# Delta-rule attention and feed-forward on one core: one join product per block, half as many fill transfers, and the Gram steps at a block's first slot

## The chip, the cores and the metric

The kernel runs on one core of a Trainium2 chip. The metric is the device time of one execution in microseconds, as the median of three runs. Five engines work side by side: TensorE (PE in the profile; its weight loads are PEld), VectorE (DVE), ScalarE (ACT), GpSimd (POOL) and SyncE (SP), which here only issues transfers.

## The reference

Four sequences of 768 steps with eight heads of size 48 go through a delta rule; its output, 3072 rows of 384, goes through a feed-forward of width 2048.

```python
for t in range(S):
    kt, vt, bt = (k_n[:, :, t], v[:, :, t], beta[:, :, t, None])
    y[:, :, t] = np.einsum('bhd,bhde->bhe', q[:, :, t], state)
    v_old = np.einsum('bhde,bhd->bhe', state, kt)
    state = state + bt[:, :, :, None] * np.einsum('bhd,bhe->bhde', kt, vt - v_old)
...
h = x @ w_in
g = np.maximum(0.01 * h, h)
return (g @ w_out).astype(np.float32)
```

## The kernel before

The 768 steps are cut into 12 blocks of 64 steps (`C`); a block holds 32 problems (8 heads x 4 sequences), handled as two groups `g` of 16. For block n the kernel does, in this order:

- `gram(n)`: products of the keys with the keys and queries (`pg`, L282) for each g. ScalarE copies the key part to `gs` (L286), from where eight transfers write it to `gd` in DRAM (L290) and two read it back as `L` (L306), problems on partitions. VectorE masks the query part into `rq` (L297) and copies the quadrant that joins the two halves of a problem into `gm` (L303).
- `inv(n)`: VectorE takes the norms from `L` (L323 to L332) and eliminates (L347, L352: some 122 small instructions) to the inverses of the two 32-step halves, tile `T`. ScalarE makes a second layout (L401, "the T copy"); transfers write both layouts to DRAM (`td` L408, `tt` L409).
- `solve(n)`: `merge_z` reads the inverses back: four transfers into `rt` (L461), and 16 fills of 16 KB that place 32x32 pieces on the diagonals of `sa` (L465) and `sb` (L468), two tiles for each g. The join product is `pz` (L436, from `gm` and `sa`), scaled to `zs` (L471), then in `merge_u` `pu` (L436, from `sb` and `zs`), copied into `rt` (L490). Then `pk` (L553), `pw` (L569), `pc` (L579, carries the state on) and `py` (L589), whose result `ys` (L591) is the block's output.
- `columns(n)`: TensorE transposes `ys` to `px` (L619); ScalarE and VectorE split it into `xh` and `xl` (L120, L121).
- `ffn(n)`: 16 slots f, each nine matmuls `ph` (L648), `gh` on ScalarE (L653), a second activation in place (L654), `gl` on VectorE (L656), and later six matmuls `po` (L638). At the block's end `po` is copied to `ob` (L668, in the same three buffers as `ys`) and stored (L671).

While the feed-forward of block n runs, `weave` traces the steps of later blocks between its slots: solve(n+1), inv(n+2) and gram. A tuple (stream, steps, a, b) spreads the steps from slot a to slot b. A scheduler then sets the final order of each engine's queue, with `behind(...)` as constraints; so the order on the engines is not the order of the source. All transfers that matter here stand in one queue, SP's, in order: one that waits holds all behind it.

Blocks 0 and 1 share one inverse and go another way. Tiles `cg` hold converted weights in block 0 and later `sa` and `sb`. `ps_a` gives four PSUM banks to all small products.

A "block" below is the stretch between two `pn` matmuls (L509), the first instruction of each solve from block 2 on; they stand at 142.06, 197.08, 245.39, ... 540.77 and 586.83 us.

Of the kernel before, what the change touches and what calls it, by code (L numbers as in the profile page):

```python
# [39 lines left out]
KQ_BUFS = 2  # L40
KT_BUFS, Q_BUFS = 2, 4
GM_BUFS = 4
YT_BUFS = 2
R0 = 64


# [1 line left out]
def delta_moe_kernel(ctx: ExitStack, tc, kq0, kqT, kv, qT, beta, cst, w_all, out, nblk):  # L48
# [86 lines left out]
    def weights():  # L135

        for f in range(NFC):
            words = raws.pop(f).bitcast(U32).rearrange("p (n two) -> p two n", two=2)  # L140
            lo, hi = words[:, 0], words[:, 1]
            g = sb.tile([P, 2 * DO], F32, tag="cg", name=f"cg{f}", bufs=CB)
            gi = g.bitcast(U32)
            with behind("S" if f < KA else "xh"):
                nc.scalar.activation(g, hi.bitcast(F32), AF.Abs)
            with behind("mask" if f < KA else f"gl{f - AG}" if f"gl{f - AG}" in mark else "x"):
                i = nc.vector.tensor_scalar(g, g, HI_MIN, HI_MAX, ALU.max, ALU.min)
            mark["work"] = i.ins
            if f + WAHEAD >= WEARLY:
                load_w(f + WAHEAD, "work")  # L150
            nc.vector.tensor_scalar(gi, gi, 3, 0x3FFFFFF8, ALU.logical_shift_left, ALU.bitwise_and)
            nc.vector.scalar_tensor_tensor(gi, hi, 0xC0000000, gi, ALU.bitwise_and, ALU.bitwise_or)
# [106 lines left out]
    def gram(n):  # L259
        need(sv, solve, n - Q_BUFS // NGR)  # L260
        kqs = []
        for g in range(NGR):
            t = sb.tile([P, GS, NPAIR, 2, C], F32, tag="kq", name=f"kq{n}_{g}", bufs=KQ_BUFS)
            kqs.append(t)
            with behind("kq"):
                for b in range(2):
                    nc.sync.dma_start(t[b * R0:b * R0 + D].rearrange("p s u x t -> p (s u x t)"), kqT[n, g, b])
        b0 = where[n][0]
        Lh[b0] = sb.tile([P, HC, HC], F32, tag="L", name=f"L{b0}", bufs=2)
        gd = dr.tile([64, HC, HC], F32, tag="gd", name=f"gd{n}")  # L270
        for g in range(NGR):
            kq = kqs[g]
            gs = sb.tile([P, 2, NPAIR, C], F32, tag="gs", name=f"gs{n}_{g}", bufs=2)
            gm[n, g] = m = sb.tile([P, NPAIR, HC], F32, tag="gm", name=f"gm{n}_{g}", bufs=GM_BUFS)

            ps = [ps_a.tile([P, 512], F32, tag="a", name=f"pg{n}_{g}_{b}") for b in range(2)]
            pv = [x.rearrange("p (u x t) -> p x u t", u=NPAIR, x=2) for x in ps]
            for p in range(NPAIR):
                for c in range(2):
                    for b in range(2):  # L280
                        r = slice(b * R0, b * R0 + D)
                        nc.tensor.matmul(ps[b][c * 64:(c + 1) * 64, p * 128:(p + 1) * 128],  # L282
                                         kq[r, c ^ b, p, 0], kq[r, c ^ b, p].rearrange("p x t -> p (x t)"),
                                         start=True, stop=True)
            for b in range(2):
                nc.scalar.copy(gs[:, b], pv[b][:, 0])  # L286
            for c in range(2):
                for e in range(2):
                    a = e * HS + g * GH + c * GU
                    nc.sync.dma_start(  # L290
                        gd[a:a + GU].rearrange("l j i -> j l i"),
                        gs[c * 64 + e * HC:c * 64 + (e + 1) * HC].rearrange("p b u t -> p (b u) t")[:, :, e * HC:(e + 1) * HC])
            qa = of("q", n, g)
            for b in range(2):
                for c in range(2):
                    r = slice(c * 64, (c + 1) * 64)
# [127 lines left out]
    def square(x, g):

        if (x, g) not in squares:
            squares[x, g] = t = sb.tile([P, NPAIR, P], F32, tag="cg", name=f"{x}{g}", bufs=CB)
            nc.vector.memset(t, 0.0)
        return squares[x, g]

    def product(n, g, name, lhs, rhs):

        ps = ps_a.tile([P, 512], F32, tag="a", name=f"{name}{n}_{g}")
        with behind("po"):
            for i in range(NPAIR):
                nc.tensor.matmul(ps[i * HC:(i + 1) * HC, 0:P], lhs[:, i], rhs[:, i], start=True, stop=True)  # L436
        return ps[:, 0:P]

    def merge_z(n, g, t):

        T, Tt = Tts[n]
        if n < 2:
            if n:
                for e in (1, 0):
                    place(n, g, e)
            gt = gm[n, g].rearrange("p c u i -> p (c u) i")
            pz = ps_a.tile([P, 512], F32, tag="a", name=f"pz{n}_{g}")
            zv = pz[:, 0:GU * HC].rearrange("p (u t) -> p u t", u=GU)
            lo = slice(R0 + HC, P)
            with behind("po"):  # L450
                for u in range(GU):
                    for h in range(2):
                        nc.tensor.matmul(zv[h * 64:h * 64 + HC, u], gt[lo, u // NPAIR * GU + h * NPAIR + u % NPAIR],
                                         t[lo, h, u // NPAIR, u % NPAIR, HC:], start=True, stop=True)
            zs[n, g] = z = sb.tile([P, 2, GU, HC], F32, tag="yt", name=f"zs{n}_{g}", bufs=YT_BUFS)
            for h in range(2):
                nc.scalar.copy(z[n * 64:n * 64 + HC, h], zv[h * 64:h * 64 + HC])
            return
        gl = slice(g * GH, (g + 1) * GH)
        for e in (1, 0):  # L460
            nc.sync.dma_start(half_of(n, g, e).rearrange("p h u i -> p (h u) i"), T[e, :, gl])  # L461
        A, B = square("sa", g), square("sb", g)
        for k in range(NPAIR):
            r = slice(k * HC, (k + 1) * HC)
            nc.sync.dma_start(A[r, :, r], Tt[gl].rearrange("(k v) i m -> k i v m", k=NPAIR)[k])  # L465
        for v in range(NPAIR):
            r = slice(v * HC, (v + 1) * HC)
            nc.sync.dma_start(B[r, :, r], T[1, :, gl].rearrange("m (k v) i -> v m k i", k=NPAIR)[v])  # L468
        pz = product(n, g, "pz", gm.pop((n, g)), A)
        zs[n, g] = z = sb.tile([P, NPAIR, HC], F32, tag="yt", name=f"zs{n}_{g}", bufs=YT_BUFS)  # L470
        nc.scalar.mul(z.rearrange("p k (m e) -> p k e m", e=2), pz.rearrange("p (k e m) -> p k e m", k=NPAIR, e=2), -1.0)  # L471
# [321 lines left out]
```

## Time and profile before

| what | value |
|---|---|
| median of 3 runs | 665.0 us (664.61 to 666.47) |
| the profiled execution | 666.35 us, of it span 664.6 us |
| busy share of the span | PE 92%, PEld 85%, DVE 68%, ACT 51%, POOL 2% |
| TensorE's granted clock, mean | 0.986 |
| largest shares of the chain that ended last | `ph` 31%, `po` 29% |
| seven blocks from 197.08 to 540.77 us | 343.69 us, PE busy in 336.47 |

The busy time is a sum over stages with different limits, so single stretches of the timeline are what counts. Successive matmuls overlap: a row's second number is a duration, and what one costs is the distance to the next one's start. A matmul in full float32 shows as two records.

### The profile page before, as it was taken

The numbers are of one execution on the slowest core, as the hardware profiler recorded it, in microseconds if no ns is written. First come the engines' busy times: TensorE is split into PE (matmuls) and PEld (weight loads), VectorE is DVE, ScalarE is ACT, GpSimd is POOL, SyncE is SP. The second block draws the span as 40 slices with busy tenths as digits, with TensorE's granted clock in tenths as the row PEclk, the third lists the DMA queues.
The fourth block names the chain that finished last, engine by engine and source line by source line (L and its number), as shares of the span: only waits on it lengthen the run. The fifth ranks groups of instructions, "written<-read, shape, count | busy, mean of one in ns | idle before, by whom it ended". The sixth has DMA issues, their size and how long they took to land.

```text
span 664.6 us, 19968 instructions
## 1 busy us (share of the span) xinstructions
PE 609.0 (92%) x7762; PEld 563.8 (85%) x7762; DVE 450.6 (68%) x2038; ACT 337.2 (51%) x903; POOL 10.7 (2%) x17
## 2 busy tenths in 40 slices
PE   5155999999979989999999999999989999999996
PEld 4154898889869989999899999999989999989996
DVE  3998999898658748749749759659659669312221
ACT  3555897334625535545546445445545445445332
POOL 6000000000000000000000000000000000000000
PEclk9996999999979999999999999999999999999999
DMA  5972972053254543542551541650650630410101
GB/s 123 332 202 64 254 231 73 14 108 58 42 107 103 104 76 71 110 85 57 111 105 36 115 105 32 122 127 3 120 116 14 126 75 7 74 27 2 25 1 24
DMA packets 125854, 59.54 MB, mean 90 GB/s; under 512 B 112704, under 2 KB 115904, under 8 KB 125760
## 3 DMA queue, kind: packets, MB, share of 16 engines
q1 hardware_dynamic: 125344, 57.74, 38.9%
q8 instruction: 61, 1.00, 0.7%
q10 hardware_dynamic: 416, 0.53, 0.4%
q14 instruction: 33, 0.27, 0.2%
HBM read 46.96 MB, written 11.27 MB: 88 GB/s over the span
## 4 chain that ended last, share of the span: by engine, by line
PE 81%; DVE 9%; ACT 3%; DMA 3%; issue 2%; SPq 2%; ACTq 0%; DVEq 0%
PE ph L648 31%; PE po L638 29%; PE pk L553 4%; PE pw L569 3%; PE py L589 3%; PE pg L282 3%; PE pc L579 2%; PE px L619 2%; DVE tmp L347 2%; DVE T L352 2%; PE wl L175 1%; DMA gd<-gs 1%; PE pu L436 1%; PE pz L436 1%; DVE rq L297 1%
## 5 line engine op out<-in xcount | busy, mean ns | idle before, releaser
L648 PE MATMUL ph<-xh,w 128*128 128x256 f32 x1152 | 249.3, 292 | 10.6 <-ACT xh L120 7.3
L648 PEld LDWEIGHTS ph<-xh,w 128*128 128x128 f32 x1152 | 192.8, 191 | 21.8 <-ACT xh L120 7.7
L638 PE MATMUL po<-w,gh 128*128 128x384 f32 x768 | 185.4, 342 | 2.9 <-ACT gh L653 2.9
L656 DVE TENSOR_TENSOR gl<-ph,gh 128x256 fp32r<-128x256 f32 x192 | 80.6, 423 | 150.6 <-ACT ph L654 145.3
L648 PE MATMUL ph<-xl,w 128*128 128x256 f32 x576 | 163.4, 285 | 3.8 <-DVE xl L121 3.8
L653 ACT ACTIVATE gh<-ph 128x256 fp32r<-128x256 f32 x192 | 73.7, 384 | 177.6 <-PE ph L648 176.0
L638 PEld LDWEIGHTS po<-w,gh 128*128 128x128 f32 x768 | 132.1, 188 | 6.2 <-ACT gh L653 4.9
L638 PE MATMUL po<-w,gl 128*128 128x384 f32 x384 | 114.4, 338 | 0.0
L648 PEld LDWEIGHTS ph<-xl,w 128*128 128x128 f32 x576 | 110.1, 191 | 5.1 <-DVE xl L121 4.4
L352 DVE TENSOR_TENSOR T<-T,tmp 128x60 f32<-128x60 f32 (+35 forms) x661 | 113.2, 208 | 1.1
L347 DVE TENSOR_TENSOR tmp<-T,L 128x60 f32<-128x60 f32 (+35 forms) x661 | 111.5, 208 | 0.5
L654 ACT ACTIVATE ph<-ph 128x256 f32<-128x256 f32 x192 | 73.2, 381 | 0.0
L638 PEld LDWEIGHTS po<-w,gl 128*128 128x128 f32 x384 | 66.1, 188 | 0.2
L297 DVE TENSOR_TENSOR rq<-pg,csb 64x256 f32<-64x256 f32 x80 | 33.9, 423 | 17.5 <-ACT gs L286 16.5
L571 ACT COPY rv<-pw 64x384 f32<-64x384 f32 x48 | 22.7, 473 | 16.3 <-PE pw L569 15.4
L555 ACT ACTIVATE rt<-pk 48x512 f32<-48x512 f32 x44 | 26.1, 593 | 8.6 <-PE pk L553 7.8
L569 PEld LDWEIGHTS pw<-rv,rt 128*64 128x64 f32 x768 | 25.1, 145 | 2.9 <-ACT ph L654 2.3
L581 ACT COPY rv<-pc 48x384 f32<-48x384 f32 x44 | 20.8, 474 | 13.3 <-PE pc L579 13.0
L589 PE MATMUL py<-rv,rq 128*64 128x48 f32 x768 | 27.0, 224 | 0.0
L569 PE MATMUL pw<-rv,rt 128*64 128x48 f32 x768 | 26.8, 230 | 0.1
L553 PEld LDWEIGHTS pk<-rt,rk 64*48 64x48 f32 x704 | 21.9, 120 | 5.3 <-issue 2.6
L120 ACT CAST xh<-px 128x256 fp32r<-128x256 f32 x36 | 12.3, 377 | 26.2 <-PE ph L648 16.4
(91 smaller groups left out, 587.7 us busy)
## 6 DMA issues: line engine op xcount, KB each, us to landing
wr<-in_w_all SPq DMA_DIRECT2D x16, 768.0 KB, 7.9
kq<-in_kqT SPq DMA_DIRECT2D x40, 192.0 KB, 3.9
L<-gd SPq DMA_DIRECT2D x20, 256.0 KB, 4.1
rk<-in_kv SPq DMA_DIRECT2D x24, 192.0 KB, 3.8
rv<-in_kv SPq DMA_DIRECT2D x24, 192.0 KB, 4.2
rq<-in_qT SPq DMA_DIRECT2D x24, 192.0 KB, 4.5
out<-ob SPq DMA_DIRECT2D x48, 96.0 KB, 2.2
gd<-gs SPq DMA_DIRECT2D x80, 32.0 KB, 1.7
```

Source lines behind the costliest of these rows:

```text
L297: nc.vector.tensor_tensor(qa[DN, c, b * NPAIR:(b + 1) * NPAIR], pv[b][r, 1], tri[r].rearrange("p (o t) -> p o t", o=1).broadcast_to([C, NP ...
L347: nc.vector.tensor_tensor(tv, t[:, :, j:j + 1].broadcast_to([P, k, w]), L[:, j, j + 1:].rearrange("p (o w) -> p o w", o=1).broadcast_to([P ...
L352: mark["steps"] = nc.vector.tensor_tensor(t, t, tv, ALU.subtract).ins
L553: nc.tensor.matmul(pv[r, u], k[DN, c, u], t[DN, c, u // NPAIR, u % NPAIR], start=True, stop=True)
L555: nc.scalar.mul(t[UP, c], pv[c * 64:c * 64 + D].rearrange("p (y v) t -> p y v t", y=2), -1.0)
L569: nc.tensor.matmul(pv[r, u], t[:, c, u // NPAIR, u % NPAIR], v[:, c, u], start=True, stop=True)
L589: nc.tensor.matmul(pv[s * C:(s + 1) * C, u * D:(u + 1) * D], qa[:, c, u], v[:, c, u], start=True, stop=True)
L638: i = nc.tensor.matmul(po[t][:, :DO], a[:, ts_], w[f], start=(f == 0 and k == 0), stop=(f == NFC - 1 and k == 2))
L648: i = nc.tensor.matmul(ph, a[f][:, cc * P:(cc + 1) * P], x[cc][e], start=(k == 0), stop=(k == 3 * NCC - 1))
L653: nc.scalar.activation(gh, ph, AF.Prelu, alpha=0.01)
L654: i = nc.scalar.activation(ph, ph, AF.Prelu, alpha=0.01)
L656: i = nc.vector.tensor_tensor(gl, ph, gh.bitcast(F32), ALU.subtract)
```

## The change

1. `product` joins both g at once: eight matmuls into one PSUM tile, `pz` and then `pu`. `zs` is one tile of both g, scaled once; the copies of `pu` into `rt` are half as many and twice as wide.
2. `sa` and `sb` become one tile each for both g (`sq0`, `sq1`), filled by eight transfers of 32 KB; they are zeroed once by ScalarE, where VectorE did it four times. Their order among SP's transfers changes.
3. `gm` holds both g, and VectorE makes it with two copies for each g, where it was four.
4. Gram(n+2) is traced at slot 0 of block n from n = 2 on (before: gram(n+3) at slot 12), and gram(3) at slot 3 of block 1; in block 1 gram(4) is no longer traced. The inverse is traced from slot 5 (before: 2), in block 1 from slot 8.

```diff
-            g = sb.tile([P, 2 * DO], F32, tag="cg", name=f"cg{f}", bufs=CB)
+            g = sb.tile([P, 2 * DO], F32, tag=f"c{f % 4}", name=f"cg{f}", bufs=1)
...
-            gm[n, g] = m = sb.tile([P, NPAIR, HC], F32, tag="gm", name=f"gm{n}_{g}", bufs=GM_BUFS)
+            if not g:
+                gm[n] = sb.tile([P, GU, HC], F32, tag="gm", name=f"gm{n}", bufs=GM_BUFS)
...
             for c in range(2):
-                for b in range(2):
-                    k = 2 * c + b
-                    nc.vector.tensor_copy(m[k * HC:(k + 1) * HC], gs[c * 64:c * 64 + HC, b, :, HC:])
+                k = 2 * g + c
+                nc.vector.tensor_copy(gm[n][k * HC:(k + 1) * HC].rearrange("p (b u) t -> p b u t", b=2), gs[c * 64:c * 64 + HC, :, :, HC:])
...
-    def product(n, g, name, lhs, rhs):
-        ps = ps_a.tile([P, 512], F32, tag="a", name=f"{name}{n}_{g}")
+    def product(n, name, pairs):
+        ps = ps_a.tile([P, 512], F32, tag="a", name=f"{name}{n}")
         with behind("po"):
-            for i in range(NPAIR):
-                nc.tensor.matmul(ps[i * HC:(i + 1) * HC, 0:P], lhs[:, i], rhs[:, i], start=True, stop=True)
-        return ps[:, 0:P]
+            for q, w, lhs, rhs in pairs:
+                nc.tensor.matmul(ps[q * HC:(q + 1) * HC, w * P:(w + 1) * P], lhs, rhs, start=True, stop=True)
+        return ps[:, 0:2 * P]
...
+        if not g:
+            A, B = square(0), square(1)
+            for k in range(4):
+                r = slice(k * HC, (k + 1) * HC)
+                nc.sync.dma_start(A[r, :, r], Tt[k * GU:(k + 1) * GU].rearrange("u i m -> i u m"))
+            for v in range(4):
+                r = slice(v * HC, (v + 1) * HC)
+                nc.sync.dma_start(B[r, :, r], T[1, :, v::4])
+            G = gm.pop(n)
+            pz = product(n, "pz", [(u % 4, u // 4, G[:, u], A[:, u]) for u in range(GU)])
...
-              (iv, NI * (n + 2 < nblk), IV if n == 0 else 2, NF), (gg, NGR * (n < 2), 0, 2),
-              (gg, NGR * (0 < n < nblk - 3), 12, 13))
+              (iv, NI * (n + 2 < nblk), IV[min(n, 2)], NF), (gg, NGR, *GG[min(n, 2)]))
...
-IV = 7
+IV, GG = (7, 8, 5), ((0, 2), (3, 4), (0, 1))
```

What the scheduler makes of it, at three places.

ScalarE, where block 1 ends and block 2 begins. Before, the copies `ob` of the finished block and `gs` of gram(4) stand ahead of `xh`:

```order
L591 COPY ys_1_2615<-py_1_2598 128x384
L668 COPY ob_0_2905<-po_0_1994 128x384
L286 COPY gs_0_2707<-pg_0_0_2709 128x256
L286 COPY gs_0_2707<-pg_0_1_2710 128x256
L668 COPY ob_1_2909<-po_1_1995 128x384
L286 COPY gs_1_2741<-pg_1_0_2743 128x256
L286 COPY gs_1_2741<-pg_1_1_2744 128x256
L120 CAST xh_0_2881<-px_0_2873 128x256
```

The same place now (lines are the changed file's: L595 is `ys`, L400 the T copy, L672 `ob`, L119 `xh`):

```order
L595 COPY ys_1_2525<-py_1_2508 128x384
L400 COPY T_2324<-T_2324 128x16x32
L672 COPY ob_0_2791<-po_0_1989 128x384
L672 COPY ob_1_2795<-po_1_1990 128x384
L119 CAST xh_0_2767<-px_0_2759 128x256
L119 CAST xh_1_2771<-px_0_2759 128x256
L119 CAST xh_2_2775<-px_1_2760 128x256
L286 COPY gs_0_2856<-pg_0_0_2858 128x256
```

`gs` moved behind the three `xh`; the T copy of inverse 3, which stood earlier, now stands ahead of both `ob`; and `ob_1` has a buffer of which it waits for no transfer, where before it waited for the store of `ob_0`.

TensorE, the Gram products `pg` of a steady block. Before, all 32 of both g stood together in the middle of a block, behind six `po`; their first rows:

```order
L638 MATMUL po_1_3801<-w_1302,gh_10_4250 128x384 x2
L638 MATMUL po_1_3801<-w_1302,gl_10_4251 128x384
L282 MATMUL pg_0_0_4429<-kq_0_4419 64x128
L282 MATMUL pg_0_1_4430<-kq_0_4419 64x128
L282 MATMUL pg_0_0_4429<-kq_0_4419 64x128
```

Now they stand at the block's end in pieces of 6, 2, 1 and 23 matmuls, between the first `ph` of the next block; the second piece, behind the first `ph`:

```order
L652 MATMUL ph_72<-xh_0_3612,w_855 128x256
L282 MATMUL pg_0_0_3697<-kq_0_3687 64x128
L282 MATMUL pg_0_1_3698<-kq_0_3687 64x128
L652 MATMUL ph_72<-xl_0_3613,w_855 128x256
L642 MATMUL po_0_2832<-w_1518,gh_15_3575 128x384 x2
L642 MATMUL po_1_2833<-w_1518,gh_15_3575 128x384 x2
L652 MATMUL ph_72<-xh_0_3612,w_855 128x256
```

The other products of a block stand as in the last blocks before the change, which have no Gram products; only `pk`, whose first matmul stood alone ahead of nine `ph`, is one piece now.

SP's queue, one steady block, from the fills to the read of `L`. Before (`L` after 17 transfers that follow the last `tt`):

```order
L461 DMA rt_82<-td_5512 32x16x32
L465 DMA sa_2199<-tt_5513 32x4x32 x3
L290 DMA gd_5286<-gs_0_5287 32x8x32 x4
L465 DMA sa_2199<-tt_5513 32x4x32
L290 DMA gd_5286<-gs_1_5321 32x8x32 x4
L468 DMA sb_2201<-td_5512 32x4x32 x2
L306 DMA L_5285<-gd_5286 64x1024 x2
L468 DMA sb_2201<-td_5512 32x4x32 x2
L461 DMA rt_83<-td_5512 32x16x32
L465 DMA sa_2223<-tt_5513 32x4x32 x4
L468 DMA sb_2225<-td_5512 32x4x32 x4
```

Now (`L` after 23 of them; two more `rt` stand just ahead, as two stood before):

```order
L465 DMA sq_2158<-td_6180 32x8x32
L462 DMA sq_2156<-tt_6181 32x8x32 x4
L465 DMA sq_2158<-td_6180 32x8x32 x2
L675 DMA out<-ob_0_6153 64x384 x2
L675 DMA out<-ob_1_6157 64x384 x2
L290 DMA gd_6211<-gs_0_6212 32x8x32 x4
L290 DMA gd_6211<-gs_1_6244 32x8x32 x4
L465 DMA sq_2158<-td_6180 32x8x32
L471 DMA rt_82<-td_6180 32x16x32
L305 DMA L_6210<-gd_6211 64x1024 x2
```

All fills that `pz` needs moved ahead of `gd`, and the four stores moved ahead of `gd` and `L`. On VectorE the norms of the next inverse, which wait for `L`, moved from the third to the sixth slot of a block.

## Rows read from the trace of the kernel before

**Rows 1.** The page's head: the span, and TensorE's busy time, share of the span and instructions.

```profile
span 664.6 us, 19968 instructions
...
PE 609.0 (92%) x7762; PEld 563.8 (85%) x7762; DVE 450.6 (68%) x2038; ACT 337.2 (51%) x903; POOL 10.7 (2%) x17
```

**Rows 2.** Busy time by stretches, cut at the `pn` matmuls: the stretch, its length in us, then each engine's busy us and instructions, the granted clock of TensorE, the share of the DMA engines and GB/s. The fourth holds seven blocks, the fifth is a block without Gram products.

```profile
142.06:197.08 55.02, 49.53 (x592) 45.21 (x592) 39.01 (x220) 24.96 (x69) 0.00 (x0) 0.94 0.38 67
344.67:392.84 48.17, 47.87 (x607) 44.95 (x607) 34.64 (x177) 24.86 (x70) 0.00 (x0) 1.00 0.42 86
392.84:441.93 49.09, 48.16 (x608) 44.92 (x607) 34.69 (x177) 24.94 (x70) 0.00 (x0) 1.00 0.44 86
197.08:540.77 343.69, 336.47 (x4244) 314.32 (x4243) 242.47 (x1233) 174.47 (x484) 0.00 (x0) 1.00 0.44 87
540.77:586.83 46.06, 45.76 (x544) 43.27 (x543) 28.48 (x156) 23.57 (x66) 0.00 (x0) 1.00 0.25 47
```

**Rows 3.** TensorE in order of time around the end of block 1: start us, us, engine, line, operation, tiles, shapes, count, and the idle time just before with what ended it.

```profile
164.57 0.43 PE L436 MATMUL pz<-sa,gm 128*32 128x128 f32 x8
...
168.16 0.43 PE L436 MATMUL pu<-sb,zs 128*32 128x128 f32 x8
...
178.39 2.70 PE L282 MATMUL pg<-kq 48*64 48x128 f32 x64
...
186.18 0.80 PE L648 MATMUL ph<-xh,w 128*128 128x256 f32 x2 [2.51 <-ACT xh L120]
188.77 0.58 PE L648 MATMUL ph<-xl,w 128*128 128x256 f32 x1 [1.80 <-DVE xl L121]
```

**Rows 4.** ScalarE in order of time, the same place; columns as in rows 3.

```profile
176.99 1.10 ACT L401 COPY T<-T 128x512 f32<-128x512 f32 x1
...
179.47 0.48 ACT L591 COPY ys<-py 128x384 f32<-128x384 f32 x1
179.84 0.48 ACT L668 COPY ob<-po 128x384 f32<-128x384 f32 x1
...
184.82 0.48 ACT L668 COPY ob<-po 128x384 f32<-128x384 f32 x1 [3.94 <-DMA out<-ob]
...
185.72 0.41 ACT L120 CAST xh<-px 128x256 fp32r<-128x256 f32 x1
```

**Rows 5.** The chain that ended last, in order of time, around the same place: start us, us, what.

```profile
182.12 2.59 DMA out<-ob
...
188.77 3.37 PE ph L648 x14
...
193.57 1.10 PE ph L648 x9
```

**Rows 6.** TensorE's waits over the whole span: engine, what waited, for what, us in total, times, longest.

```profile
PE pz L436 <- DMA sa<-tt: 3.2, 2, 1.8
```

**Rows 7.** TensorE in order of time in block 0, where Gram products stand in pieces; columns as in rows 3.

```profile
127.17 0.66 PE L282 MATMUL pg<-kq 48*64 48x128 f32 x14
127.76 0.38 PE L648 MATMUL ph<-xh,w 128*128 128x256 f32 x1
128.07 0.43 PE L282 MATMUL pg<-kq 48*64 48x128 f32 x2
128.43 0.38 PE L648 MATMUL ph<-xl,w 128*128 128x256 f32 x1
```

**Rows 8.** TensorE in a steady block: the piece of `pk` that stands alone, and the Gram products in one row; columns as in rows 3.

```profile
256.28 0.31 PE L553 MATMUL pk<-rt,rk 64*48 64x64 f32 x2
256.51 0.39 PE L648 MATMUL ph<-xh,w 128*128 128x256 f32 x1
...
276.70 1.98 PE L282 MATMUL pg<-kq 48*64 48x128 f32 x64
278.61 0.38 PE L648 MATMUL ph<-xh,w 128*128 128x256 f32 x1
```

**Rows 9.** VectorE in order of time: the first and the last instruction of one steady inverse, with 122 elimination instructions, norms, `gl` and `rv` between them; columns as in rows 3.

```profile
392.04 0.12 DVE L323 TENSOR_SCALAR sr<-L 128x32 uint32<-128x32 uint32 x1
...
419.00 0.17 DVE L352 TENSOR_TENSOR T<-T,tmp 128x8 f32<-128x8 f32 x1
```

**Rows 10.** SP's queue in order of time in a steady block: start us, us of issuing, engine, line, transfer, count.

```profile
371.88 1.46 SPq L408 DMA_DIRECT2D td<-T  x3
...
386.49 1.12 SPq L306 DMA_DIRECT2D L<-gd  x2
...
391.21 1.85 SPq L468 DMA_DIRECT2D sb<-td  x4
```

**Rows 11.** The chain that ended last, near the end of block 2: start us, us, what.

```profile
237.62 3.27 DMA gd<-gs
```

**Rows 12.** DMA issues: transfer, count, KB each, median us from issue to landing.

```profile
L<-gd SPq DMA_DIRECT2D x20, 256.0 KB, 4.1
...
gd<-gs SPq DMA_DIRECT2D x80, 32.0 KB, 1.7
```

**Rows 13.** Groups by line, engine, operation and shape: count, busy us and mean ns of one.

```profile
L490 ACT COPY rt<-pu 32x128 f32<-32x128 f32 x80 | 20.4, 256 | 4.1 <-PE pu L436 2.4
...
L303 DVE COPY gm<-gs 32x128 f32<-32x128 f32 x80 | 17.4, 218 | 1.3
...
L428 DVE MEMSET sa<- 128x512 f32 x2 | 1.0, 485 | 0.1
```

More of the change, by code (lines that the diff above doesn't have):

```diff
@@ L42 @@
 GM_BUFS = 4
-YT_BUFS = 2
 R0 = 64
@@ L422, in delta_moe_kernel, with square @@
     squares = {}
[L424 to L429, printed above, removed]
-    def product(n, g, name, lhs, rhs):
-        ps = ps_a.tile([P, 512], F32, tag="a", name=f"{name}{n}_{g}")
+    def square(x):
+        if x not in squares:
+            squares[x] = t = sb.tile([P, GU, P], F32, tag=f"c{x}", name=f"sq{x}", bufs=1)
+            nc.scalar.mul(t, eye.rearrange("p (o t) -> p o t", o=1).broadcast_to(list(t.shape)), 0.0)
+        return squares[x]
+    def product(n, name, pairs):
+        ps = ps_a.tile([P, 512], F32, tag="a", name=f"{name}{n}")
         with behind("po"):
-            for i in range(NPAIR):
-                nc.tensor.matmul(ps[i * HC:(i + 1) * HC, 0:P], lhs[:, i], rhs[:, i], start=True, stop=True)
-        return ps[:, 0:P]
+            for q, w, lhs, rhs in pairs:
+                nc.tensor.matmul(ps[q * HC:(q + 1) * HC, w * P:(w + 1) * P], lhs, rhs, start=True, stop=True)
+        return ps[:, 0:2 * P]
     def merge_z(n, g, t):
@@ L454, in merge_z @@
                                          t[lo, h, u // NPAIR, u % NPAIR, HC:], start=True, stop=True)
-            zs[n, g] = z = sb.tile([P, 2, GU, HC], F32, tag="yt", name=f"zs{n}_{g}", bufs=YT_BUFS)
+            zs[n, g] = z = sb.tile([P, 2, GU, HC], F32, tag="gs", name=f"zs{n}_{g}", bufs=2)
             for h in range(2):
@@ L458, in merge_z @@
             return
-        gl = slice(g * GH, (g + 1) * GH)
-        for e in (1, 0):
[L461 to L471, printed above, removed]
+        if not g:
[8 more added lines that the diff above has]
+            pz = product(n, "pz", [(u % 4, u // 4, G[:, u], A[:, u]) for u in range(GU)])
+            zs[n] = z = sb.tile([P, GU, HC], F32, tag="yt", name=f"zs{n}", bufs=1)
+            nc.scalar.mul(z.rearrange("p x (m e) -> p x e m", e=2), pz.rearrange("p (x e m) -> p x e m", x=GU, e=2), -1.0)
+        for e in (1, 0):
+            nc.sync.dma_start(half_of(n, g, e).rearrange("p h u i -> p (h u) i"), T[e, :, g * GH:(g + 1) * GH])
     def merge_u(n, g, t):
-        z = zs.pop((n, g))
         if n < 2:
+            z = zs.pop((n, g))
             gm.pop((n, g))
@@ L487, in merge_u @@
             return
-        pu = product(n, g, "pu", z, square("sb", g))
-        for k in range(NPAIR):
-            nc.scalar.copy(t[R0:R0 + HC, k // 2, k % 2, :, HC:], pu[k * HC:(k + 1) * HC].rearrange("p (v t) -> p v t", v=NPAIR))
+        if not g:
+            z, B = zs.pop(n), square(1)
+            zs[n, "u"] = product(n, "pu", [(k, w, z[:, 4 * w + k], B[:, 2 * k + w]) for w in range(2) for k in range(4)])
+        pu = zs[n, "u"]
+        for h in range(2):
+            k = 2 * g + h
+            nc.scalar.copy(t[R0:R0 + HC, h, :, :, HC:], pu[k * HC:(k + 1) * HC].rearrange("p (y v t) -> p y v t", y=2, v=NPAIR))
     LD = 2
@@ L722 @@
 KA, KB, WB = 4, 3, 12
-CB = 4
-IV = 7
+IV, GG = (7, 8, 5), ((0, 2), (3, 4), (0, 1))
 LL, AG = 2, 6
```

## The prediction

> **What bounds the kernel now.** I read the page's head first: TensorE is busy in 609.0 of 664.6 us [rows 1]. So most of what the change does on other engines can be worth nothing, and the question is where TensorE waits and what it is made to do. I then cut the span at the `pn` matmuls, one in each block, and took the busy time of each stretch [rows 2]. The seven blocks from 197.08 to 540.77 us take 343.69 us, of which TensorE is busy in 336.47: 49.1 us a block, in single blocks 48.17 or 49.09. The block without Gram products takes 46.06. At most 7 us are to be had in all seven by taking away waits. The stretch from 142.06 to 197.08 is another matter: 55.02 us, 5.5 of them idle, and a granted clock of 0.94. There I read TensorE and ScalarE in order of time. The first `ph` of block 2 starts at 186.18 and the row of them really runs only from 188.77 on [rows 3]. The reason is on ScalarE: the second copy `ob` waits 3.94 us for the store of the first and starts at 184.82, and `xh`, which `ph` needs, stands behind it at 185.72 [rows 4]. The chain of waits says the same: 2.59 us of `out<-ob`, and then 14 `ph` in 3.37 us, 0.24 each, against nine in 1.10 us, 0.12 each, a little later [rows 5]. [...]
>
> **The change, part by part.**
>
> *End of block 1.* The order of ScalarE shows `ob_0` and `ob_1` together, no longer with the store between them, then the three `xh`, and `gs` behind. Before, `ys_1` ends at 179.95 [rows 4]. Behind it I put the T copy (1.10), two `ob` (0.48 each) and the first `xh` (0.41) [rows 4], 2.5 us in all, and about 1 us until TensorE has done its `px` and the `po` between them: `ph` runs from about 183.5, where it ran from 188.77. That gains 5.2, and 1.7 if the clock then stays up. Against it, gram(4), which TensorE did between 178.39 and 181.1, before `px` [rows 3], now falls partly behind it: half of its 64 records (1.0 us) and two pieces (0.8). Also, the join of block 2 is one product now. Before, `pz` of the second g stood at 164.57 and its `pu` at 168.16 [rows 3]; now all of `pz` waits for all fills, but these are issued at once. VectorE is spared four memsets of 0.485 us and, for the eight `gm` copies of 0.218, four of double width (estimate 0.28, since the fixed part is paid once) [rows 13]: 2.5 us in the stretch in which the inverse of block 2 runs on it. I take 1.3 us of that for the solve. Sum: 5.2 + 1.7 - 1.8 + 1.3 = 6.4 us gained; bounds 2 (the T copy late, see the rivals) and 8.
>
> *Gram products in pieces.* TensorE's order in a steady block is that of the block of 46.06 us [rows 2], plus the Gram products in four pieces, less the lone `pk`. In one row they take 1.91 us for 64 records, 0.03 each [rows 8], and about 0.2 for going in and out. For a small piece there are two prices. A piece of 14 records takes 0.59 us where 14 x 0.03 = 0.42 is work; a piece of two starts 0.31 us after the `ph` before it started (a `ph` takes 0.12) and holds the next for 0.36 us, where 0.06 is work [rows 7]: 0.2 to 0.5 us a piece. Two of the three new pieces have four and two records, so I take 0.45; the lone `pk` is let go at 0.35 (0.23 from its start to the next `ph` [rows 8], and the way in). A block is then 46.06 + 2.1 + 1.35 - 0.35 = 49.2 us, seven of them 344.2: 0.5 us lost. At 0.2 each it is 48.6 a block, 3.7 gained.
>
> [...]
>
> *Fills.* Eight transfers fewer spare SP 8 x 0.46 us a block [rows 10], and the fills of `pz` now stand ahead of `gd`. The wait of `pz` for `sa`, 3.2 us in two waits [rows 6], should be gone; it lies inside the 343.69, so the 49.2 above already holds that gain. Elsewhere the spared issuing is hidden under TensorE.
>
> *Narrow work on other engines.* Eight `pu` copies of 0.256 us become four of double width; ScalarE has room, and VectorE's `gm` copies likewise [rows 13]. I cost them at nothing: TensorE's `ph` and `po` cover them. If that cover were gone, they would give about 1 us a block. The zeroing of two tiles on ScalarE in block 0 falls among its weight copies: 0 to 2 us lost; VectorE's relief there, 0 to 2 gained. I take 0.5 gained.
>
> *The last two blocks.* They have no Gram products and lose the lone `pk`: 2 x 0.35 = 0.7 gained.
>
> *What the later Gram costs.* The inverse now starts behind a Gram of the same block, so it is a ring: `L` lands, VectorE inverts, the layouts go to DRAM, and behind them in SP's queue stand the fills, the stores, `gd` and the next `L`. The inverse took from 392.04 to 419.17 [rows 9], 27.1 us. From the first `td` to the second `L` it was 371.88 to about 387.0 [rows 10], 15.1 us; now six transfers more stand between, 6 x 0.46 = 2.8. `L` lands 4.1 us after its issue [rows 12]. Ring: 27.1 + 15.1 + 2.8 + 4.1 = 49.1 us, against 49.2 for TensorE's block. So it just fits. The cover is thin: by the same rows `L` lands 7 to 8 us into a block, and TensorE first waits when `L` comes some 9.5 us in, because `pw` needs `rv`, which VectorE scales behind the norms.
>
> Sum: 6.4 - 0.5 + 0.5 + 0.7 = 7.1 us. The profiled execution took 666.35 us, 1.35 above the median of 665.0; it would be 659.3, and the median **658 us**.
>
> **The rivals.**
>
> *The ring binds (slower).* `gd` lands 1.7 us after its issue by its median [rows 12], but 3.27 us in the block before 245.39 [rows 11]. If that is the rule when the stores stand just ahead of it, the ring is 50.6 us. Each of seven blocks is then 1.4 us longer, 10 in all, and the gain of block 1 does not make up for it when the T copy is late too: 668 us. For it: the sum of the ring is as long as the block. Against it: part of the 27.1 us are `gl` that wait for TensorE, and the first blocks have 1.5 to 2 us in hand. It decides from `L` 9.5 us into a block.
>
> *The gain at block 1 is lost to the T copy (no change).* ScalarE now has that copy ahead of both `ob` and `xh`, and it waits for inverse 3, which starts later than before (slot 8). If inverse 3 ends 4 us later than I think, `ph` starts at 187.5 and 2 to 3 us are left: 662.5 us. For it: VectorE does 36 of the elimination instructions behind the last `gl` of block 1. Against it: TensorE's last slot there comes some 5 us before `ys_1`, about the time that these 36 take.
>
> *The pieces cost nothing.* [...] Blocks are then 46.06 + 2.1 - 0.35 = 47.8 us, 1.35 better than in my sum, 9.5 in seven: 648.5. For it: the `ph` on both sides of a piece don't need its result. Against it: the pieces of block 0 [rows 7] cost more than their work. [...]
>
> **How the numbers follow.** Mine 0.50, the ring 0.20, the T copy 0.18, the free pieces 0.12. A measurement of this kernel can tell about 0.3%, 2 us, from no change: 663 to 667 is the same. Faster: 0.50 + 0.12 + a third of the T copy's 0.18 = 0.68. Same: the other two thirds and a little of the ring, 0.15. Slower: the rest of the ring, 0.17. The range, from 650 (pieces at 0.2 us and the full 8 us of block 1 give 652, the free pieces lie just under it) to 668 (the ring), leaves out about 2 in 10; mine alone is 654 to 662.
>
> **What would show it.** The stretch between the `pn` at 142 and the next falls from 55.0 to about 48.6 us, with no wait of `ob` for `out` and no 0.24 us `ph` behind it; where that stays near 53, the T copy stood in the way, and ScalarE's wait for VectorE there says so. Steady blocks are 49.2 us; at 47.8 the pieces were free, at 50.5 the ring binds, and then VectorE's first norm waits for `L<-gd` in each block and TensorE for `rv` or `gl`. `pz` waits for no fill. I am wrong altogether if a wait grows that I have at nothing: `pz` or `pu` for fills that are 32 KB now, or `po` for `gl` behind VectorE's masks at a block's end.

## The result, and the profile after

The changed kernel takes 669.17 us (median of five runs, 668.75 to 672.19) against 664.61 us beside it: a ratio of 1.0077 (95% interval 1.0049 to 1.0104). It is slower by 0.8%, where 658 us and faster was forecast.

The head of its page answers to [rows 1]: TensorE is busy 4.1 us longer, in a span 2.8 us longer.

```profile
span 667.4 us, 19795 instructions
...
PE 613.1 (92%) x7762; PEld 566.9 (85%) x7762; DVE 442.0 (66%) x1994; ACT 331.7 (50%) x855; POOL 10.7 (2%) x17
```

Next come the stretches of both kernels, with the columns of [rows 2]. First those of before that were not shown: from the start to the first steady `pn`, block 2, the six blocks behind it, and the end.

```profile
0.00:142.06 142.06, 105.20 (x1718) 91.57 (x1718) 125.21 (x396) 84.80 (x202) 10.72 (x17) 0.96 0.57 161
197.08:245.39 48.31, 48.01 (x608) 44.81 (x607) 33.86 (x173) 24.91 (x70) 0.00 (x0) 1.00 0.51 97
245.39:540.77 295.38, 288.46 (x3638) 269.50 (x3637) 208.62 (x1060) 149.56 (x415) 0.00 (x0) 1.00 0.42 85
586.83:664.60 77.77, 71.99 (x671) 69.43 (x670) 15.38 (x36) 29.43 (x86) 0.00 (x0) 0.99 0.05 11
```

The changed kernel: the start, block 1, block 2, the first of the six blocks, all six, the block without Gram products, and the end.

```profile
0.00:144.41 144.41, 105.15 (x1718) 91.99 (x1718) 124.68 (x400) 86.82 (x204) 10.72 (x17) 0.94 0.57 156
144.41:193.15 48.74, 48.74 (x593) 44.97 (x592) 36.81 (x195) 24.65 (x64) 0.00 (x0) 1.00 0.43 81
193.15:246.12 52.97, 49.19 (x607) 45.45 (x607) 33.76 (x172) 24.05 (x65) 0.00 (x0) 1.00 0.47 88
246.12:295.84 49.72, 48.85 (x607) 45.33 (x607) 33.55 (x172) 24.06 (x65) 0.00 (x0) 1.00 0.41 83
246.12:544.44 298.32, 293.09 (x3637) 271.98 (x3637) 202.30 (x1032) 144.70 (x385) 0.00 (x0) 1.00 0.43 84
544.44:590.07 45.63, 45.33 (x543) 43.18 (x542) 29.11 (x160) 22.75 (x61) 0.00 (x0) 1.00 0.27 51
590.07:667.40 77.33, 71.57 (x671) 69.33 (x670) 15.37 (x36) 28.74 (x81) 0.00 (x0) 0.98 0.07 14
```

| stretch | before | after | difference | forecast |
|---|---|---|---|---|
| start to the first `pn` | 142.06 | 144.41 | +2.35 | -0.5 |
| block 1 | 55.02 | 48.74 | -6.28 | -6.4 |
| block 2 | 48.31 | 52.97 | +4.66 | +0.86 |
| six blocks behind it | 295.38 | 298.32 | +2.94 | -0.36 |
| block without Gram, and end | 123.83 | 122.96 | -0.87 | -0.7 |
| span | 664.6 | 667.4 | +2.8 | -7.1 |

(The forecast gave 49.17 us to each of the seven blocks from block 2 on.) The gain at block 1 came in full. Three losses stand against it, each with its own wait.

**The six blocks.** TensorE in order of time at a block's end (columns of [rows 3]):

```profile
292.50 0.86 PE L642 MATMUL po<-w,gh 128*128 128x384 f32 x4
294.23 0.39 PE L652 MATMUL ph<-xh,w 128*128 128x256 f32 x1 [0.87 <-DVE gl L660]
```

and VectorE at the same place:

```profile
289.06 1.73 DVE L297 TENSOR_TENSOR rq<-pg,csb 64x256 f32<-64x256 f32 x4
290.80 0.58 DVE L302 COPY gm<-gs 32x256 f32<-32x256 f32 x2
291.39 1.73 DVE L297 TENSOR_TENSOR rq<-pg,csb 64x256 f32<-64x256 f32 x4
293.14 0.58 DVE L302 COPY gm<-gs 32x256 f32<-32x256 f32 x2
293.75 0.76 DVE L660 TENSOR_TENSOR gl<-ph,gh 128x256 fp32r<-128x256 f32 x2
```

The masks and copies of the moved Gram stand 4.6 us in a row on VectorE. The two `gl` behind them could have started at about 291.2 and 292.3, when ScalarE was through with their `ph` (second activations of 0.38 us from 290.85 and 291.93). TensorE has done its last `po` at 293.36 and waits 0.87 us until the first `gl` is done, which reads the tile (`hbank`) that the next `ph` is written to. Neither `gl` passes the masks here: the first starts at 293.75, 2.5 us after its `ph` was ready.

**Block 0.** ScalarE, TensorE and SP around 80 us, one line or two of each:

```profile
80.44 0.73 ACT L456 COPY zs<-pz 32x256 f32<-32x256 f32 x2
85.31 0.36 ACT L456 COPY zs<-pz 32x256 f32<-32x256 f32 x1 [3.46 <-DMA gd<-gs]
...
82.37 1.10 PE L484 MATMUL pu<-zs,T 32*32 32x32 f32 x32
86.97 1.11 PE L484 MATMUL pu<-zs,T 32*32 32x32 f32 x32 [3.50 <-ACT zs L456]
...
77.37 2.73 SPq L290 DMA_DIRECT2D gd<-gs  x4
```

A line of the change that the cut diff does not hold explains it: `zs` of the first two blocks was given the buffers of `gs`.

```diff
-            zs[n, g] = z = sb.tile([P, 2, GU, HC], F32, tag="yt", name=f"zs{n}_{g}", bufs=YT_BUFS)
+            zs[n, g] = z = sb.tile([P, 2, GU, HC], F32, tag="gs", name=f"zs{n}_{g}", bufs=2)
```

So `zs` must wait until the stores `gd` have read the `gs` in its buffer, and those run among the weight loads of block 0: they land 4.7 to 7.3 us after their issue there, against a median of 1.7 us in the kernel before [rows 12]. ScalarE and TensorE stand still, and in the slice from 80 to 90 us the granted clock is 0.73 (1.00 before).

**Block 2.** TensorE, then SP's queue at the end of block 1:

```profile
197.54 0.65 PE L435 MATMUL pz<-sq,gm 128*32 128x128 f32 x16 [1.77 <-issue]
202.84 0.64 PE L435 MATMUL pu<-sq,zs 128*32 128x128 f32 x16 [1.14 <-DMA sq<-td]
...
183.03 2.30 SPq L675 DMA_DIRECT2D out<-ob  x2
185.37 0.58 SPq L407 DMA_DIRECT2D td<-T  x1
186.06 2.43 SPq L675 DMA_DIRECT2D out<-ob  x2
188.53 0.59 SPq L407 DMA_DIRECT2D td<-T  x1
189.16 0.62 SPq L408 DMA_DIRECT2D tt<-T  x1
189.88 2.09 SPq L290 DMA_DIRECT2D gd<-gs  x4
195.47 0.45 SPq L462 DMA_DIRECT2D sq<-tt  x1
```

Inverse 3, which starts later in block 1 now, ends so late that its layouts `td` and `tt` are issued between the stores `out`, which wait for `ob`; its fills come behind them and behind `gd`, and `pz` and `pu` wait for them. For `pz` that is inferred, as its row names no releaser: the last `sq<-tt` is issued at 195.47, these transfers land 1.9 us after their issue here (median), and `pz` starts at 197.54. The two waits are 2.9 us of the 3.25 by which block 2 is longer than a steady block.

**Block 1.** ScalarE and TensorE, where [rows 3, 4] had the wait of 3.94 us and a `ph` at 188.77 (46.71 us behind the block's `pn`, now 39.71):

```profile
179.72 1.09 ACT L400 COPY T<-T 128x512 f32<-128x512 f32 x1 [0.46 <-DVE T L351]
...
182.81 0.48 ACT L672 COPY ob<-po 128x384 f32<-128x384 f32 x1 [1.54 <-PE px L623]
183.19 0.38 ACT L119 CAST xh<-px 128x256 fp32r<-128x256 f32 x1
...
184.12 0.51 PE L652 MATMUL ph<-xh,w 128*128 128x256 f32 x2
```

### The profile page after: what moved, and what is told of

It reads as the page before. It is cut to its first block, busy times and chain, and to the rows that moved or that the text cites. A ratio compares the mean times of both kernels' runs of the same rounds, so it can differ in the third digit from the quotient of the medians.

```text
span 667.4 us, 19795 instructions
## 1 busy us (share of the span) xinstructions
PE 613.1 (92%) x7762; PEld 566.9 (85%) x7762; DVE 442.0 (66%) x1994; ACT 331.7 (50%) x855; POOL 10.7 (2%) x17
## 4 chain that ended last, share of the span: by engine, by line
PE 77%; DVE 11%; DMA 5%; issue 3%; SPq 1%; ACT 1%; ACTq 0%; DVEq 0%
PE ph L652 30%; PE po L642 27%; PE pw L573 3%; PE pk L557 3%; PE py L593 3%; PE pc L583 3%; DVE rq L297 2%; PE pg L282 2%; PE px L623 2%; DVE T L351 2%; DVE tmp L346 2%; DVE gm L302 1%; PE wl L174 1%; DMA gd<-gs 1%; DMA rv<-in_kv 1%
## 5 line engine op out<-in xcount | busy, mean ns | idle before, releaser
L652 PE MATMUL ph<-xl,w 128*128 128x256 f32 x576 | 165.2, 287 | 2.0 <-DVE xl L120 2.0
L351 DVE TENSOR_TENSOR T<-T,tmp 128x60 f32<-128x60 f32 (+35 forms) x661 | 111.5, 208 | 0.6
L282 PE MATMUL pg<-kq 48*64 48x128 f32 x640 | 32.4, 279 | 0.0
L120 DVE TENSOR_TENSOR xl<-px,xh 128x256 fp32r<-128x256 f32 x36 | 14.1, 419 | 22.5 <-ACT xh L119 22.5
L282 PEld LDWEIGHTS pg<-kq 48*64 48x64 f32 x640 | 22.2, 133 | 7.7 <-issue 4.3
```

The lines of the kernel that those rows point to most:

```text
L351: mark["steps"] = nc.vector.tensor_tensor(t, t, tv, ALU.subtract).ins
L652: i = nc.tensor.matmul(ph, a[f][:, cc * P:(cc + 1) * P], x[cc][e], start=(k == 0), stop=(k == 3 * NCC - 1))
```

## Experiments

All ratios are to the kernel before, run on the same chip.

**The buffers of `zs`.** A third buffer under the shared tag:

```diff
-... tag="gs", name=f"zs{n}_{g}", bufs=2)
+... tag="gs", name=f"zs{n}_{g}", bufs=3)
-... tag="gs", name=f"gs{n}_{g}", bufs=2)
+... tag="gs", name=f"gs{n}_{g}", bufs=3)
```

> The changed kernel with a third buffer under the tag that gs and, for the first two blocks, zs share. Theory: in block 0 TensorE stands 3.50 us before the second pu because ScalarE's zs of block 1 needs a buffer from which the stores gd still read (ScalarE waits 3.46 us for gd<-gs), and the clock falls behind that stop. With a third buffer this wait is gone, the first steady pn stands at about 141 us where it is at 144.4, and the time falls by 2.5 to 4.5 us, from 669.2 to about 665.5; the later blocks keep 49.7 us. Rival: block 0 is held by the weight conversions on ScalarE and VectorE anyway, and the stop only moves: the first pn stays behind 143.5 and less than 1.5 us are gained.

Measured 665.28 us, 1.0002 (0.9984 to 1.002). The first `pn` stands at 141.53, the blocks stay at 49.72. ScalarE now makes all four `zs` without a stop, and both `pu` are one row:

```profile
80.03 1.50 ACT L456 COPY zs<-pz 32x256 f32<-32x256 f32 x4
...
81.95 2.01 PE L484 MATMUL pu<-zs,T 32*32 32x32 f32 x64
```

The theory holds: the wait is gone, and the first `pn` comes 2.9 us earlier in the profiled execution. The size is less sure than the cause, as this stretch differs between executions. In the four profiles of this document with two buffers and the new table at this place, the first `pn` stands at 144.18 to 147.04 us; in the three with a third buffer it stands at 138.98 to 141.53. The two groups do not overlap, and their means are 5.1 us apart.

**The row on VectorE.** The `gm` copies to the engine that has time there:

```diff
-nc.vector.tensor_copy(gm[n][k * HC:(k + 1) * HC]...
+(nc.scalar.copy if n > 3 else nc.vector.tensor_copy)(gm[n][k * HC:(k + 1) * HC]...
```

> The changed kernel with the four gm copies of gram(4) and later made by ScalarE instead of VectorE; nothing else changes place. Theory: at each steady block's end TensorE waits 0.87 us for a gl which stands on VectorE behind eight rq and four gm instructions (4.6 us in a row). Without the gm copies (1.16 us) that gl ends 1.1 us earlier and the wait is gone: steady blocks 48.85 us instead of 49.72, seven or eight of them, 6 us in all, 663 us. Rival: gl is late because of ph and not because of the row on VectorE, or ScalarE, with 1.2 us more to do, is late with gh instead: blocks stay at 49.5 or more.

Measured 662.44 us, 0.9954 (0.9934 to 0.9973). The first steady block, and VectorE and TensorE at its end:

```profile
245.51:294.10 48.59, 48.59 (x607) 45.37 (x606) 32.49 (x168) 25.61 (x69) 0.00 (x0) 1.00 0.41 84
...
288.45 3.48 DVE L297 TENSOR_TENSOR rq<-pg,csb 64x256 f32<-64x256 f32 x8
291.95 0.76 DVE L660 TENSOR_TENSOR gl<-ph,gh 128x256 fp32r<-128x256 f32 x2
...
291.89 0.87 PE L642 MATMUL po<-w,gh 128*128 128x384 f32 x4
292.59 0.28 PE L652 MATMUL ph<-xh,w 128*128 128x256 f32 x1
```

TensorE is busy for all of the block, and its order in a steady block is the same as in the changed kernel. Nothing but the copies moved, so the row on VectorE was the cause, and it cost 1.15 us a block (49.72 to 48.57 in five of the six blocks). That is more than the 0.87 us of the wait in the rows, since an idle time starts at the end of a matmul and matmuls overlap: from the last `po` to the next `ph` it was 1.73 us (292.50 to 294.23) and is 0.70 (291.89 to 292.59), and the `ph` after the idle time held its successor for 0.22 us instead of 0.12. The sixth block, of 49.61 us, has another wait, 6.3 us behind its `pn`:

```profile
348.97 0.65 PE L435 MATMUL pu<-sq,zs 128*32 128x128 f32 x16 [0.97 <-ACT ph L658]
```

The ScalarE instruction named there was done at 348.35. The last fill of `pu` was issued at 345.94, 3.3 us into the block, against at most 2.4 us in the other blocks from 294.10 on; so the wait is probably for this fill, though the row does not name it.

**The late inverse in block 1.**

```diff
-IV, GG = (7, 8, 5), ((0, 2), (3, 4), (0, 1))
+IV, GG = (7, 5, 5), ((0, 2), (3, 4), (0, 1))
```

> The changed kernel with the inverse in block 1 traced from slot 5, as in the steady blocks, instead of slot 8. Theory: in the stretch from 193 to 246 us pz (1.77 us) and pu (1.14 us) wait for fills that are late because inverse 3 ends late, so that its layouts td and tt stand in SP's queue between the stores out, which wait for ob, and its fills behind those. With the inverse earlier both waits go: the stretch takes about 50 us instead of 52.97, the time falls by 2.5 to 3 us to about 666.4. Rival: the fills are late because they stand behind the stores gd of gram(4) in the queue, which are there all the same: the stretch stays above 52 us.

Measured 668.73 us, 1.0058 (1.0035 to 1.0081). Block 2 falls from 52.97 to 51.33, but block 1 grows from 48.74 to 49.94. In block 2 the wait of `pz` falls from 1.77 to 0.48 us and that of `pu`, 1.14 us, is gone. So the late inverse is a cause, but curing it in this way only moves 1.2 of the 1.6 us to block 1, where TensorE now waits 0.88 us for `gl`. Block 2 stays at 51.33, between the theory and the rival: beside the 0.48 us TensorE waits 0.79 us there for `rt`, read back from `td` behind the fills, and 0.88 us for `gl` as in every steady block.

**One half at a time.** First the joint product with the old table of slots:

```diff
-(iv, ..., IV[min(n, 2)], NF), (gg, NGR, *GG[min(n, 2)]))
+(iv, ..., IV[0] if n == 0 else 2, NF), (gg, NGR * (n < 2), 0, 2),
+(gg, NGR * (0 < n < nblk - 3), 12, 13))
```

> The changed kernel with the old table of slots (gram(n+3) at slot 12, the inverse from slot 2): the joint product, the eight fills and the wide gm copies alone. Theory: the gain at the end of block 1 is the table's, so it goes: ob waits about 3.9 us for the store of ob again and the stretch from the first to the second pn is 53 to 55 us. The late gl at the blocks' ends is the table's too: steady blocks 48.2 to 49.1 us. Block 0 keeps the wait for gd (the first pn at 144). In all 664 to 667 us. Rival: the joint product costs by itself, since pz waits for all fills: steady blocks above 49.5 us, 672 us or more.

Measured 657.6 us, 0.9873 (0.9829 to 0.9917), below the expectation. The six steady blocks, and VectorE in one of them, with the same row of masks and copies that stands at a block's end in the changed kernel:

```profile
246.44:533.64 287.20, 285.39 (x3638) 268.97 (x3637) 204.40 (x1036) 145.53 (x385) 0.00 (x0) 1.00 0.45 88
...
276.85 1.75 DVE L297 TENSOR_TENSOR rq<-pg,csb 64x256 f32<-64x256 f32 x4 [1.33 <-ACT gs L286]
278.61 0.58 DVE L302 COPY gm<-gs 32x256 f32<-32x256 f32 x2
```

47.87 us a block (287.20 / 6), 1.4 less than before. In the middle of a block the same 4.6 us on VectorE cost TensorE nothing. I was wrong on block 1: its stretch is 48.79 us, though the table is the old one. ScalarE's order there became `gs`, `xh`, `ob`, so `xh` no longer stands behind the store. The wait of `pu` in block 0 is longer, 5.7 us (the first `pn` at 147.0).

Then the table with two products:

```diff
-(iv, ..., IV if n == 0 else 2, NF), (gg, NGR * (n < 2), 0, 2),
-(gg, NGR * (0 < n < nblk - 3), 12, 13))
+(iv, ..., IV[min(n, 2)], NF), (gg, NGR, *GG[min(n, 2)]))
```

> The kernel before with the new table of slots alone: two products, sixteen fills and eight narrow gm copies as before. Theory: the table is what costs. A steady block pays the Gram pieces (0.7 us, the distance of gm_act4 to merge_only) and the wait for gl behind VectorE's row at the block's end, which is longer with eight gm copies, and two more pieces of pz and pu: 50 to 51.5 us where it was 49.1; block 0 keeps 142 us, since zs has its own buffers. In all 668 to 680 us. Rival: the table costs only with the joint product: steady blocks stay at 49.1 to 49.5, and the time at 660 to 665 us.

Measured 681.72 us, 1.0261 (1.0233 to 1.029), above the expectation. The first `pn` is at 138.38 and block 1 takes 49.30 us, but the blocks behind it take 50.73 to 55.51. TensorE's waits, which all stand behind the first `pn` (columns of [rows 6]):

```profile
PE ph L648 <- DVE gl L656: 10.9, 8, 1.5
PE pz L436 <- DMA sa<-tt: 6.0, 3, 2.4
```

So the table costs 17 us by itself, and the joint product, which gains 7 us under the old table, gains 12.5 under the new one. Either alone takes the stall out of block 1.

**The ring.** The row on VectorE mended as above, and the Gram traced one slot later:

```diff
-IV, GG = (7, 8, 5), ((0, 2), (3, 4), (0, 1))
+IV, GG = (7, 8, 5), ((0, 2), (3, 4), (1, 2))
```

> gm_act4 with the Gram step of a steady block traced at slot 1 instead of 0: its products stand in three pieces (6, 2 and 24) instead of four (6, 2, 1 and 23). Theory: each piece beyond the first costs TensorE 0.24 us (0.7 us for three), so a steady block falls from 48.57 to about 48.3 us. By the price in the prediction (0.45) it falls to 48.1; if pieces cost nothing, it stays at 48.57. The other bound of the run: a new wait at the block's end, which the waits would name.

One run, 679.06 us, so its rows carry the reading rather than its time. Two blocks of it; VectorE's first norm in each, which starts when `L` has landed; and TensorE in the second:

```profile
247.71:295.77 48.06, 48.06 (x607) 45.12 (x606) 32.47 (x169) 25.62 (x68) 0.00 (x0) 1.00 0.42 83
347.14:401.03 53.89, 50.78 (x607) 47.76 (x606) 32.50 (x169) 25.82 (x68) 0.00 (x0) 0.94 0.41 82
...
256.42 0.19 DVE L322 TENSOR_SCALAR sr<-L 128x32 uint32<-128x32 uint32 x1 [2.75 <-DMA L<-gd]
360.55 0.19 DVE L322 TENSOR_SCALAR sr<-L 128x32 uint32<-128x32 uint32 x1 [7.44 <-DMA L<-gd]
...
362.54 0.58 PE L652 MATMUL ph<-xh,w 128*128 128x256 f32 x1 [3.11 <-DVE gl L660]
```

The time was to be about that of the kernel with the copies on ScalarE, and it is 17 us more: the bound named in the expectation came. With `L` 8.7 us into the block (256.42 - 247.71) the block takes 48.06 us; with 9.9 it is 49.1, with 11.9 it is 51.4, with 13.4 it is 53.9. VectorE waits in the norms for `L`, `gl` stands behind them, TensorE waits for `gl`, and the granted clock falls to 0.94. This is the ring of the first rival: from one issue of `L` to the next (250.93, 302.17, 354.96, 405.15 us) it takes 50.2 to 52.8 us. The edit moved SP's queue too: in the block from 347.14 on, three reads of `kq` are issued ahead of `L`, which stood behind it with the Gram at slot 0. How much of the delay is theirs was not tested. The block without the wait gives the price of pieces: TensorE busy in 48.06 us with three, 48.57 to 48.59 with four, 47.57 (285.39 / 6) in one row: 0.2 to 0.5 us for each piece more.

**Both mends in the changed kernel.** The edits of the first two experiments together.

> The changed kernel, with its new table, with both mends: a third buffer for gs and zs, and the gm copies of gram(4) and later on ScalarE. Theory: the two causes lie in different stretches and add: 669.2 less 3.9 (gs3) less 6.7 (gm_act4), 658.6 us, faster than before by 0.9%. What is left against merge_gs3 is the pieces in the steady blocks (0.7 us each, 5 in all) and the late fills of block 2 (1 us). Rival: VectorE and ScalarE meet in block 0 or 2 and the sum is under 9 us: above 660.

Measured 657.09 us, 0.9894 (0.987 to 0.9918). They add, and the first `pn` stands at 139.81. In one of the six blocks `L` comes 9.5 us behind the `pn`, and the block still takes 48.61.

**The joint product with the third buffer,** old table: the edits of the first and the fourth experiment together.

> The joint product, the eight fills and the wide gm copies with the old table of slots, as in merge_only, and a third buffer for gs and zs. Theory: the wait of the second pu in block 0 (5.7 us in merge_only, for zs, which waits for a gs buffer) is gone, and nothing else changes: the first pn at 141.5 us instead of 147.0, the time 652 us (657.6 less 5.5), faster than before by 1.9%. Rival: as in gs3, where 2.9 us of a wait of 3.5 came back, part is taken by the conversions behind it: 654 us.

Measured 655.93 us, 0.988 (0.985 to 0.991). The first `pn` is at 139.13, 7.9 us earlier, but block 1 takes 52.38: `pz` waits 3.06 us there for fills and 1.87 in block 2. The fills of block 1 are issued no later than without the third buffer, from 11.2 us behind the `pn` against 11.4. But the scheduler's order has changed: `pz` stands one slot earlier on TensorE, 80 matmul records behind the `pn` where it was 95. A slot takes 2.1 us there, most of the wait, and behind it a `ph` starts 0.21 us after the one before it (155.51 to 155.72), where it is 0.12 from 158.33 on; the granted clock is 0.97 from 140 to 191 us. It is the rival's result by another way: the time came back at the fills, not at the conversions.

**A version with the shorter half of each.** The third buffer, the new table up to gram(4), the old one behind it:

```diff
-(iv, ..., IV[min(n, 2)], NF), (gg, NGR, *GG[min(n, 2)]))
+(iv, ..., (7, 8, 2)[min(n, 2)], NF), (gg, NGR * (n < 3), *GG[min(n, 2)]),
+(gg, NGR * (1 < n < nblk - 3), 12, 13))
```

> The changed kernel with the third buffer for gs and zs, the new table in blocks 0 and 1 and for gram(4) (block 2, slot 0), and the old one from there on (gram(n+3) at slot 12, the inverse from slot 2). Theory: each half is taken where it was the shorter one: blocks 0 to 2 as in the run with both mends (the second steady pn at 188.6 us, the third at 239.2), the blocks after it as in merge_gs3 (47.87 us each, 123 us from the pn at the end of the seven to the end). 239.2 + 6 x 47.87 + 123.0 = 649.4 us of span, some 651.5 us, faster than before by 1.9%. Rival: with gram(4) and gram(5) in the same block that block waits (52 us or more) and nothing is gained on merge_gs3's 655.9.

Measured 651.62 us, 0.9806 (0.9772 to 0.9841): faster than both kernels. Start, block 1, block 2 and the six blocks:

```profile
0.00:138.98 138.98, 103.33 (x1718) 90.78 (x1718) 124.80 (x402) 86.26 (x204) 10.72 (x17) 0.98 0.59 163
138.98:187.71 48.73, 48.73 (x592) 44.95 (x591) 36.73 (x194) 24.65 (x64) 0.00 (x0) 1.00 0.41 77
187.71:238.29 50.58, 48.12 (x607) 44.95 (x606) 34.04 (x176) 23.97 (x65) 0.00 (x0) 1.00 0.48 94
238.29:525.49 287.20, 285.39 (x3637) 268.98 (x3637) 203.71 (x1033) 145.35 (x385) 0.00 (x0) 1.00 0.46 89
```

Two variants did worse. With gram(4) at slot 12 of block 1 (`NGR * (n < 2)` and `NGR * (0 < n < nblk - 3)` in the lines above):

> As h1, but gram(4) stays at slot 12 of block 1, so that every block from 1 on has its Gram at slot 12. Theory: block 0 as in the run with both mends (first pn at 139.8), the stretch of block 1 48.8 to 50 us (Gram in one row, but TensorE's way to px as in merge_gs3), block 2 as in merge_gs3 with the fills late by 1.9 us, 50 to 51 us; 650 to 653 us. Rival: block 1 loses the 3 us that merge_gs3 loses there (52.4 us, pz for fills): 655 us.

Measured 657.01 us, 0.9874 (0.984 to 0.9908): block 1 takes 48.87, but block 2 takes 56.22, as `pz` waits 5.4 us for fills there, which neither the theory nor the rival had. And the joint product with the third buffer, with gram(3) at slot 12 of block 0 (`NGR * (n < 1)` at 0, `NGR * (n < nblk - 3)` at 12):

> merge_gs3 with gram(3) at slot 12 of block 0 instead of slot 0 of block 1. In merge_gs3 pz waits 3.06 us in block 1 and 1.87 us in block 2 for fills, as the inverses before them end late. Theory: an earlier L gives an earlier inverse 3 and its fills, so the wait of block 2 goes (1.9 us) and that of block 1, which hangs on inverse 2, stays: 654 us. Rival: VectorE is full in block 0 and block 1 (40 us busy of 51), the inverse is not earlier and the Gram in block 0 costs its 2 us: 656 to 658 us.

Measured 656.12 us, 0.9863 (0.9829 to 0.9898): no gain, as the rival said. But the parts came out otherwise: block 1 loses its wait for fills (48.11 us instead of 52.38), which the theory had staying, and block 2 takes 56.10, with 5.1 us for a `gl` that stands behind the norms of an `L` that lands late.

## Why the prediction was wrong

- **End of block 1: right.** 6.28 us against 6.4. Counted from the block's `pn`, as block 0 ended later than before, `ph` comes 7.0 us earlier (46.71 to 39.71), where 5.2 and 1.3 were said; from there to the next `pn` it takes 9.03 us instead of 8.31, where 0.1 more was said. Each part is within 0.6 us, and the two errors cancel: that the sum is so close is luck. The 1.7 us that the sum has for the clock is 14 x 0.12 from [rows 5], and no run shows what lets the clock fall or keeps it up. What the runs show is that the granted clock is 0.51 from 188.77 to 192.14 us in the kernel before, where 16 `ph` (the chain names 14 of them) start 0.21 us apart, and 1.00 from 184.10 to 193.15 in the changed kernel, where a `ph` behind another starts 0.12 us after it. Each half of the change alone takes the stall away (48.79 and 49.30 us).
- **"Narrow work on other engines" at nothing: the step that failed in the steady blocks.** The cover was named ("TensorE's `ph` and `po` cover them"), its price too ("about 1 us a block"), and the last sentence on what would make the forecast wrong named the wait. But I took the cover for given, because it holds in the middle of a block, and did not set the moved row of 4.6 us beside what TensorE has to do at a block's end. It measured 1.15 us a block. The price of the wide `gm` copy was right: 0.284 us for 256 columns in the changed kernel, said 0.28, against 0.218 for 128 before.
- **Gram in pieces: right mechanism, too dear.** Three pieces more made a block 0.70 us longer (48.57 against 47.87) where the sum had 1.35. The third rival had a piece free; it costs 0.23 us here (0.70 / 3). The rival's 47.8 us was also not consistent: where pieces are free, the lone `pk` gives nothing back, and the sum is 46.06 + 2.1 = 48.2. The error in the pieces hid half of the one above: a block came out at 49.72, said 49.17.
- **Fills: wrong at one place.** The steady waits of `pz` went, as said. For block 2 I used the steady block and left out that inverse 3 starts at slot 8; its fills come late and block 2 takes 52.97, 3.8 more than said: 2.9 are the waits of `pz` and `pu`, 0.55 is what every steady block lost too, and the rest is busy time. The rival on the T copy asked the right question (is inverse 3 late?) of the wrong reader: the T copy waited 0.46 us, the fills were late.
- **Block 0: a term that is missing.** 0.5 gained was said, 2.35 lost. The shared tag stands in the change, though not in the cut diff, and a buffer's next writer waits for the stores that read it: 3.46 us here. It got no term at all. With the third buffer the first `pn` comes 0.53 us earlier than in the kernel before, as was said; but as that stretch differs by 2 to 3 us between executions, the agreement says little.
- **The last two blocks: right,** 0.87 us against 0.7.
- **The ring: not what happened, but the size was right.** In the changed kernel VectorE has `L` by 6.6 to 8.5 us into a block, and it costs nothing. One slot later it binds: nothing at 8.7 us, 1.0 us at 9.9 (said: from 9.5). The rival's 668 us left out its own second condition: the ring alone gives 658 + 10, and with the T copy 4 us late too it would be some 672.

In the profiled executions the span missed its forecast of 657.5 us by 9.9: 2.85 us in block 0, 3.8 in block 2 and 3.3 in the six blocks, with 0.1 more and 0.2 less in the others.

## What to carry to other kernels

Work moved off the critical engine's path is not free at every place: the same 4.6 us on VectorE cost TensorE nothing in the middle of a block, where it had other work, and 1.15 us a block at the end. Ask of every moved row what stands behind it on its engine and who waits for that, most of all at a seam between blocks. Follow each buffer that a change lets two tiles share to whoever still reads it, transfers included (3.46 us here). And take the transition blocks one by one: a steady block's price says nothing about the first block whose input comes from a step that was moved.

## What was not expected

The two halves of the change did not add: -7 us for the joint product, +17 for the table, +4.6 together. And work added to ScalarE (1.55 us of busy time in the first steady block) made the kernel faster, since it took a wait for VectorE off TensorE.
